# A conformer block on one core: the passage behind attention reordered, and its last token tile normalised from PSUM in halves

## The chip, the cores and the metric

The kernel runs on one core of one Trainium2 chip. The metric is the device time of one execution in microseconds (us); smaller is better. The profile of a kernel is taken from one execution of it. Its span is about 4 us shorter than the device time of the same execution, so I compare spans with spans and times with times.

## The reference

Input x is 2 x 4000 tokens of 512 features; the inner width of the feed-forwards is 2048, and the depthwise convolution has 3 taps. Norms have no learned factors.

```python
h = _layernorm(x);  h = _silu(h @ w_ff1_a) @ w_ff1_b;  x1 = x + 0.5 * h
h = _layernorm(x1); q, k, v = h @ w_q, h @ w_k, h @ w_v
p = _softmax(jnp.einsum('btd,bsd->bts', q, k) * scale)
x2 = x1 + jnp.einsum('bts,bsd->btd', p, v) @ w_o
h = _layernorm(x2) @ w_pw1
h = a * _sigmoid(b)                      # a, b: the two halves of h
dc = depthwise convolution of h over 3 tokens
dc = (dc - mu) / jnp.sqrt(var + 1e-05)   # mu, var over all tokens
x3 = x2 + _silu(dc) @ w_pw2
h = _layernorm(x3); h = _silu(h @ w_ff2_a) @ w_ff2_b; x4 = x3 + 0.5 * h
return _layernorm(x4)
```

The statistics of the convolution run over all tokens. So nothing behind them can start before the last tokens have left attention, and this is what makes a **passage** between attention and the second feed-forward in which TensorE has little work to choose from.

## The kernel before

Tokens are handled in chunks of four tiles of 127. TensorE (PE) does all products, and transposes the normed tiles. A norm is: statistics and mean on VectorE (DVE), variance plus EPS on DVE, power of -0.5 on GpSimd (POOL), a shift on DVE (minus mean times factor, one column), and the norm itself on ScalarE (ACT) or DVE. PSUM is the memory that PE's sums go to, in banks. The "gate" is the product of a and the sigmoid of b, on one engine, with copies of its edge columns for the neighbouring chunk (the halo); the "swish" is the silu behind the convolution, on ACT. SyncE (SP) and ACT issue the transfers (DMA).

```python
def copy_o(self, W):                       # attention output, PSUM to SBUF, 4 copies
    for dc in range(DC):
        if dc % 2: DVE tensor_copy(self.OT[:, dc, 0:W], self.Yb[dc][:, 0:W])
        else:      ACT Copy of the same
# ... project(g, ti): 4 matmuls of one tile from OT, then the residual on DVE

def gate(eng):                             # in conv_a, for the last but one chunk
    self.S.op(eng, lambda e: e.tensor_tensor(out=out, in0=asb, in1=th, op=ALU.mult), ...)
    self.halo_left(t, jj); self.halo_right(t, jj)      # two one-column copies on POOL
if jj < DC - 1:
    return gate("POOL")
return lambda: gate("DVE")

def ln_factor(self, sl, ti):
    # DVE: va = mv + EPS;  POOL: rs = va ** -0.5
```

The passage itself, first half (attention's end to the last tile's products) and second half (to the feed-forward):

```python
for jj in range(self.KEEP, DC - 2):
    self.conv_b(tail, jj)
    self.conv_a(tail, jj)
def prepare(ti):
    self.project(last, ti)
    if ti == 0: self.conv_b(tail, DC - 2)
    if ti == 2: self.conv_a(tail, DC - 2)
for ti in self.ln_tiles(last, ..., prepare, ("ACT", "ACT", "DVE", "DVE")):
    if ti == TPC - 3:
        self.conv_b(tail, DC - 1)
        gate = self.conv_a(tail, DC - 1)
# ... transposes of the normed tiles, gate(), copies of the depthwise products
# ... loop over the last chunk's channel groups
self.conv_shift(DC - 2); self.swish(0, 2)
self.pw2_x(0, all_t[0:2], banks[0:2])
finish(DC - 1)                             # depthwise products and statistics, last group
self.conv_shift(DC - 1); self.swish(0, 3)
# ... norms of the first chunk
ybanks = [ybank() for _ in all_t]
self.pw2_x(1, all_t, ybanks)               # five matmuls for each of four tiles
self.pw2(1, all_t, ybanks, False)
x_away(1, 0, "ACT"); x_away(1, 1, "DVE"); x_away(0, 0, "ACT")
for k in range(2):
    self.transpose_pair(k, 0, ("ACT", "DVE")[k], ybanks[k], 0)
# ... the other x_away copies, then the feed-forward
```

The end of the last chunk, and the end of the program. A second version of the program stands behind a branch and is not taken in these runs:

```python
for ti in range(token_tiles(c)):           # in ff_last
    for f in range(FC):                    # 16 matmuls of 512 columns
        self.ff_second(f, ti, *blocks[f], f == FC - 1)
    self.residual(self.Yb[ti][0:TILE, :], self.b_Y[ti], c * TPC + ti, 0.5)
    self.ln_stats(c, sl, ti); self.ln_mean(sl, ti); self.ln_factor(sl, ti)
    self.ln_norm(c, sl, ti, self.osb[0][:, ti, :], self.b_osb[0][ti], "DVE")
    self.store_out(c, self.osb[0], self.b_osb[0], ti, ti + 1, ("SP", "ACT"))
# ... in build()
self.program(False)
self.wait_out()
with nc.If(fits < 1):
    S.barrier(); self.program(True); self.wait_out()
```

The first weights are loaded in this order at the start (each piece of `w_a` is 256 KB):

```python
for k in range(self.NWA):
    self.load_wa(i["w_ff1_a"], k, "SP")
    self.load_wb(i["w_ff1_b"], 2 * k, 2 * k + 2)
```

Of the kernel before, what the change touches and what calls it, by code (L numbers as in the profile page):

```python
# [246 lines left out]
class Conformer:  # L247
# [19 lines left out]
    def memory(self):  # L267
# [70 lines left out]

        self.P = [C.view(oP + s * 1024, CHUNK) for s in range(self.NP)]
# [45 lines left out]

        ns = self.LN_SLOTS
# [10 lines left out]
        self.st = [small(TPC * 6, parts=TILE).rearrange("p (t s) -> p t s", t=TPC) for _ in range(ns)]  # L397
# [3 lines left out]
        self.va = [small(TPC, parts=TILE) for _ in range(ns)]  # L401
        self.b_va = [[Buf("va") for _ in range(TPC)] for _ in range(ns)]
# [9 lines left out]
        self.b_nr1 = Buf("nr1")  # L412
        self.onef = small(1)
# [196 lines left out]
    def ln_stats(self, c, sl, ti, src=None):  # L610
        x, b_x = self.tokens(c, ti, src)
        self.S.op("DVE", lambda e: e.bn_stats(self.st[sl][:, ti, :], x), reads=[b_x], writes=[self.b_st[sl][ti]])  # L612

    def ln_aggr(self, sl, n, shift=False):
        S = self.S
        for ti in range(n):
            S.op("DVE", lambda e, ti=ti: e.bn_aggr(self.mv[sl][:, ti, :], self.st[sl][:, ti, :]),
                 reads=[self.b_st[sl][ti]], writes=[self.b_mv[sl][ti]])
        S.op("DVE", lambda e: e.tensor_scalar(self.va[sl][:, 0:n], self.mv[sl][:, 0:n, 1], EPS, None, ALU.add),  # L619
             reads=self.b_mv[sl], writes=self.b_va[sl])  # L620
        S.op("POOL", lambda e: e.tensor_tensor(out=self.rs[sl][:, 0:n], in0=self.va[sl][:, 0:n],  # L621
                                               in1=self.neghalf[0:TILE, 0:n], op=ALU.pow),
             reads=self.b_va[sl] + [self.b_neghalf], writes=self.b_rs[sl])
# [98 lines left out]
    def ln_factor(self, sl, ti):  # L722
        S = self.S
        S.op("DVE", lambda e: e.tensor_scalar(self.va[sl][:, ti:ti + 1], self.mv[sl][:, ti, 1:2], EPS, None, ALU.add),
             reads=[self.b_mv[sl][ti]], writes=[self.b_va[sl][ti]])
        S.op("POOL", lambda e: e.tensor_tensor(out=self.rs[sl][:, ti:ti + 1], in0=self.va[sl][:, ti:ti + 1],  # L726
                                               in1=self.neghalf[0:TILE, ti:ti + 1], op=ALU.pow),
             reads=[self.b_va[sl][ti], self.b_neghalf], writes=[self.b_rs[sl][ti]])
# [64 lines left out]
    def ff_last(self, c, old):  # L793

        S, late = self.S, FC - self.NP
        blocks = []
# [11 lines left out]
        sl = self.nxt("ln", self.LN_SLOTS)  # L808
        for ti in range(token_tiles(c)):
            for f in range(FC):  # L810
                self.ff_second(f, ti, *blocks[f], f == FC - 1)
            self.residual(self.Yb[ti][0:TILE, :], self.b_Y[ti], c * TPC + ti, 0.5)
            self.ln_stats(c, sl, ti)
            self.ln_mean(sl, ti)
            self.ln_factor(sl, ti)
            self.ln_norm(c, sl, ti, self.osb[0][:, ti, :], self.b_osb[0][ti], "DVE")
            self.store_out(c, self.osb[0], self.b_osb[0], ti, ti + 1, ("SP", "ACT"))

# [178 lines left out]
    def copy_o(self, W):  # L997
        for dc in range(DC):
            if dc % 2:
                self.S.op("DVE", lambda e, dc=dc: e.tensor_copy(self.OT[:, dc, 0:W], self.Yb[dc][:, 0:W]),  # L1000
                          reads=[self.b_Y[dc]], writes=[self.b_OT[dc]])
            else:
                self.act(self.OT[:, dc, 0:W], self.Yb[dc][:, 0:W], AF.Copy, [self.b_Y[dc]], [self.b_OT[dc]])

    def project(self, g, ti):
# [3 lines left out]
        n, t0 = r.stop, ti * TILE - r.start  # L1009
        for dc in range(DC):  # L1010
            self.mm(ps[0:n, :], self.OT[:, dc, t0:t0 + n], self.Wvo[:, dc, :],
                    dc == 0, dc == DC - 1, [self.b_OT[dc], self.b_Wvo], b_ps)
# [11 lines left out]
    def finish_queries(self, g, done):  # L1024
        self.copy_o(width(g))
# [22 lines left out]
    def conv_a(self, t, jj):  # L1048
# [6 lines left out]
        if t == NCK - 2 and jj >= self.KEEP:  # L1055
# [10 lines left out]
            if jj < DC - 1:  # L1066
                return gate("POOL")
            return lambda: gate("DVE")
# [221 lines left out]
    def constants(self):  # L1290
        S = self.S
        S.op("POOL", lambda e: e.memset(self.neghalf, -0.5), writes=[self.b_neghalf])
        S.op("DVE", lambda e: e.memset(self.zero, 0.0), writes=[self.b_zero])  # L1293
        S.op("POOL", lambda e: e.memset(self.hl, 0.0), writes=self.b_hl)
        for j in range(TPC):
            S.op("DVE", lambda e, j=j: e.memset(self.ltm[j], 0.0), writes=[self.b_ltm[j]])
        S.op("POOL", lambda e: e.memset(self.onef, 1.0), writes=[self.b_onef])
        S.op("DVE", lambda e: e.memset(self.XT[SHARED][HALF - 32:HALF], 0.0), writes=[self.bx[SHARED]])
# [8 lines left out]
    def program(self, any_score):  # L1307
# [95 lines left out]
        for jj in range(self.KEEP, DC - 2):  # L1403
            self.conv_b(tail, jj)
            self.conv_a(tail, jj)

        def prepare(ti):
            self.project(last, ti)
            if ti == 0:
                self.conv_b(tail, DC - 2)  # L1410
            if ti == 2:
                self.conv_a(tail, DC - 2)

        for ti in self.ln_tiles(last, self.nxt("ln", self.LN_SLOTS), prepare, ("ACT", "ACT", "DVE", "DVE")):
            if ti == TPC - 3:
                self.conv_b(tail, DC - 1)
                gate = self.conv_a(tail, DC - 1)
# [4 lines left out]
        gate()  # L1422
# [8 lines left out]
        def finish(cc):  # L1431
            for t in (last, tail):
                f, copy = self.depthwise(t, cc)
                f()
                copies.append(copy)
            self.conv_scale(cc)
# [25 lines left out]
        self.conv_shift(DC - 2)  # L1462
        self.swish(0, 2)
# [3 lines left out]
        finish(DC - 1)  # L1467
# [15 lines left out]
        for ti in self.ln_tiles(0, self.nxt("ln", self.LN_SLOTS), None, ("ACT", "ACT", "DVE", "DVE"), x):  # L1483
            pass
        ybanks = [ybank() for _ in all_t]
        self.pw2_x(1, all_t, ybanks)
        self.pw2(1, all_t, ybanks, False)
# [7 lines left out]
        x_away(1, 1, "DVE")  # L1495
        x_away(0, 0, "ACT")
        for k in range(2):
            self.transpose_pair(k, 0, ("ACT", "DVE")[k], ybanks[k], 0)
        for t, ti, eng in ((0, 1, "ACT"), (0, 2, "DVE"), (1, 2, "ACT"), (0, 3, "DVE"), (1, 3, "ACT")):
# [78 lines left out]
```

## Time and profile before

| | before |
|---|---|
| median of the runs beside the changed kernel | 2047.64 us (4 runs, 2047.34 to 2047.93) |
| span of the profile | 2043.1 us |
| PE busy | 99% |
| idle PE time in the passage (1512 to 1556) | 5.8 us |
| last matmul's end to the end of the span | 5.8 us |

PE is busy in all but 13.5 us of 2043.1, so a change that takes no matmul away can win only part of these. The prediction below shows the lines of the page, the passage and the tail, and how they are read.

### The profile page before, as it was taken

The page shows a single profiled execution, that of the slowest core. Times are in us where ns is not written, and L with a number is a line of the kernel's source. Part 1 is how long each engine was busy: PE and PEld are TensorE (multiplying, and loading weights), DVE is VectorE, ACT ScalarE, POOL GpSimd, SP SyncE. Part 2 cuts the span into 40 slices and gives each one's busy share as a digit, 9 for nine tenths or more (in the row PEclk, how much of TensorE's full clock was granted, in tenths as well). Part 3 has the DMA queues.
Part 4 walks back from the last instruction along what each step waited for, and adds up shares of the span by engine and source line. Part 5 has one row for each costly group of instructions (what it writes and reads, how often), then busy time and mean ns, then how long its engine had stood idle before and what let it go on. Part 6 is the DMA issues. An engine that isn't in the chain of part 4 may idle for free.

```text
span 2043.1 us, 24518 instructions
## 1 busy us (share of the span) xinstructions
PE 2029.6 (99%) x9649; PEld 1028.9 (50%) x9649; DVE 1093.0 (54%) x2264; ACT 743.9 (36%) x1274; POOL 109.4 (5%) x236
## 2 busy tenths in 40 slices
PE   9999999999999999999999999999999999999998
PEld 5555555554444444445444444444445555555555
DVE  4244443334556667666766676667674444434434
ACT  3433333333333333333333333333345443443433
POOL 1000000000000000000000000000011000000000
PEclk9999999999999999999999999999999999999999
DMA  8222245320101111114421111111143111111111
GB/s 185 52 62 62 53 101 124 96 70 8 26 16 29 24 31 26 29 24 96 106 55 23 28 29 29 24 28 29 39 135 93 32 31 42 32 31 41 28 35 38
DMA packets 253121, 104.42 MB, mean 51 GB/s; under 512 B 193412, under 2 KB 252487, under 8 KB 252999
## 3 DMA queue, kind: packets, MB, share of 16 engines
q1 hardware_dynamic: 252751, 102.61, 21.1%
q8 instruction: 78, 1.28, 0.3%
q14 instruction: 44, 0.36, 0.1%
q10 hardware_dynamic: 248, 0.18, 0.0%
HBM read 33.77 MB, written 23.34 MB: 28 GB/s over the span
## 4 chain that ended last, share of the span: by engine, by line
PE 97%; DVE 1%; issue 0%; POOL 0%; DMA 0%; ACT 0%; POOLq 0%; SPq 0%; DVEq 0%; ACTq 0%
PE s L500 55%; PE y L500 42%; DVE work L612 0%; DVE wff L1177 0%; POOL work L726 0%; ACT work L550 0%; DVE xt L753 0%; DMA work<-work 0%; DMA xt<-in_x_dram 0%; DVE work L634 0%; POOL work L1186 0%; DVE work L547 0%; DVE wff L1071 0%; DVE work L920 0%; DVE work L719 0%
## 5 line engine op out<-in xcount | busy, mean ns | idle before, releaser
L550 ACT ACTIVATE work<-s 128x508 bf16<-128x508 f32 (+3 forms) x1060 | 621.7, 587 | 1212.8 <-PE s L500 1208.3
L500 PE MATMUL s<-work,wff 128*128 128x508 bf16 (+5 forms) x2624 | 628.2, 371 | 2.3 <-DVE work L547 1.8
L500 PE MATMUL s<-work,keys 128*128 128x508 bf16 (+1 forms) x2048 | 516.7, 374 | 0.1
L500 PE MATMUL y<-work,keys 128*128 128x508 bf16 (+2 forms) x2048 | 504.3, 373 | 0.4 <-DVE work L1000 0.4
L500 PE MATMUL y<-wff,work 128*127 128x512 bf16 x1992 | 501.2, 379 | 0.0
L920 DVE TENSOR_TENSOR work<-work 128x508 f32<-128x508 f32 (+2 forms) x496 | 334.6, 675 | 279.9 <-ACT work L550 278.8
L500 PEld LDWEIGHTS s<-work,wff 128*128 128x128 bf16 x2624 | 252.2, 98 | 278.6 <-issue 6.2
L500 PEld LDWEIGHTS y<-wff,work 128*127 128x127 bf16 x1992 | 273.7, 137 | 171.4
L500 PEld LDWEIGHTS s<-work,keys 128*128 128x128 bf16 x2048 | 199.5, 98 | 231.9 <-issue 0.6
L500 PEld LDWEIGHTS y<-work,keys 128*128 128x128 bf16 (+1 forms) x2048 | 193.5, 97 | 234.0 <-issue 6.2
L753 DVE SCALAR_TENSOR_TENSOR xt<-y,xt 127x512 bf16<-127x512 f32 x126 | 78.5, 683 | 360.1 <-PE y L500 360.1
L612 DVE BATCH_NORM_STATS2 work<-xt 127x6 f32<-127x512 bf16 x312 | 197.3, 680 | 6.3 <-DMA xt<-in_x_dram 6.2
L500 PE MATMUL s<-work 128*127 128x512 bf16 (+3 forms) x776 | 197.0, 378 | 2.2 <-DVE work L1293 1.2
L621 POOL TENSOR_TENSOR work<-work 127x4 f32<-127x4 f32 (+1 forms) x76 | 76.5, 1007 | 1133.0 <-DVE work L619 1133.0
L500 PEld LDWEIGHTS s<-work 128*127 128x127 bf16 (+1 forms) x776 | 94.9, 124 | 76.9 <-issue 3.7
L634 DVE TENSOR_SCALAR work<-xt,work 127x512 bf16<-127x512 bf16 x307 | 110.8, 407 | 26.2 <-POOL work L621 22.9
L753 DVE SCALAR_TENSOR_TENSOR xt<-s,xt 127x512 bf16<-127x512 f32 x55 | 38.0, 692 | 144.6 <-PE s L500 144.6
L753 DVE SCALAR_TENSOR_TENSOR xt<-s,work,xt 127x512 bf16<-127x512 f32 x64 | 48.0, 751 | 32.1 <-PE s L500 31.5
L1075 DVE SCALAR_TENSOR_TENSOR wff<-wff,s 128x508 bf16<-128x508 f32 (+1 forms) x57 | 38.7, 679 | 41.6 <-PE s L500 41.4
L550 ACT ACTIVATE wff<-s 128x508 f32<-128x508 f32 (+1 forms) x67 | 39.5, 591 | 55.1 <-PE s L500 55.1
L550 ACT ACTIVATE work<-keys,work 128x508 bf16<-128x508 bf16 (+1 forms) x68 | 52.3, 775 | 1.4 <-DVE work L1191 1.3
L1156 POOL COPY wff<-wff 128x1 bf16<-128x1 bf16 x56 | 10.4, 187 | 635.3 <-DVE wff L1075 632.8
(83 smaller groups left out, 424.5 us busy)
## 6 DMA issues: line engine op xcount, KB each, us to landing
keys<-keysd SPq DMA_DIRECT2D x62, 128.0 KB, 2.3
keysd<-work SPq DMA_DIRECT2D x14, 448.0 KB, 3.2
out_dram<-work SPq DMA_DIRECT2D x14, 448.0 KB, 3.2
dcvd<-wff SPq DMA_DIRECT2D x48, 127.0 KB, 1.7
keys<-dcvd SPq DMA_DIRECT2D x12, 508.0 KB, 4.9
xt<-in_x_dram SPq DMA_DIRECT2D x13, 448.0 KB, 4.8
wff<-in_w_ff_a_dram SPq DMA_DIRECT2D x16, 256.0 KB, 5.4
work<-work SPq DMA_TRANSPOSE x208, 2.5
```

Source lines behind the costliest of these rows:

```text
L500: self.S.op("PE", lambda e: e.matmul(out, lhsT, rhs, start=start, stop=stop, **kw), reads=reads, writes=[bank], inc=stop if inc is None el ...
L550: return self.S.op("ACT", lambda e: e.activation(out, in_, func, **kw), reads=reads, writes=writes)
L612: self.S.op("DVE", lambda e: e.bn_stats(self.st[sl][:, ti, :], x), reads=[b_x], writes=[self.b_st[sl][ti]])
L621: S.op("POOL", lambda e: e.tensor_tensor(out=self.rs[sl][:, 0:n], in0=self.va[sl][:, 0:n], in1=self.neghalf[0:TILE, 0:n], op=ALU.pow), rea ...
L634: self.S.op("DVE", lambda e: e.tensor_scalar(out, x, self.mv[sl][:, ti, 0:1], self.rs[sl][:, ti:ti + 1], ALU.subtract, ALU.mult), reads=[b ...
L753: self.S.op("DVE", lambda e: e.scalar_tensor_tensor(out=self.XT[g][rows], in0=ps[rows], scalar=scalar, in1=self.XT[g][rows], op0=ALU.mult, ...
L920: S.op("DVE", lambda e, p=p, n=n, acc=acc: e.tensor_tensor(out=acc, in0=acc, in1=self.P[p][0:n, 0:W], op=ALU.add), reads=[self.b_P[p], sel ...
L1075: self.S.op("DVE", lambda e: e.scalar_tensor_tensor(out=out, in0=th, scalar=1.0, in1=ps[:, 0:W], op0=ALU.add, op1=ALU.mult), reads=[b_ps, ...
L1156: S.op("POOL", lambda e: e.tensor_copy(self.G[gs][:, jj, 0:1], self.G[gp][:, jj, CHUNK:CHUNK + 1]), reads=[self.b_G[gp][jj]], writes=[self ...
```

## The change

The intent is to fill PE's idle time at both ends of the passage and behind the last matmul. It has five parts.

1. **EPS goes into the statistics.** The six numbers that DVE's statistics give for a tile are followed by three constant ones, which stand for no element but are to add D times EPS to the sum of squares in the operation that forms mean and variance. So the variance is to have EPS in it, and the 91 adds on DVE that the profile of before counts go.
2. **First half.** The copies of the attention output are split at 127 columns, so that the first tile is projected ahead of the gates' products; of the two gates on POOL the first stays, behind the first tile's power ("factor"), and the second goes to DVE, where the third was already.
3. **Second half.** The shift of the third channel group, which waits for POOL (DVE idles 0.73 us at 1542.28 before), stands behind a statistics operation instead of ahead of it.
4. **Second half.** Only three tiles of the second chunk are multiplied ahead of the transposes; the fourth tile's five matmuls come behind them, while their copies run. The first transposes get a spare PSUM bank.
5. **Tail.** PE adds twice the residual through an identity matrix, so that the last tile's sum is twice x4, whose norm is the same with four times EPS. The tile is done in two halves of 256 columns, with ACT's square root and DVE's reciprocal in place of POOL's power; one half is normed by DVE and one by ACT, from PSUM.

```diff
-    def copy_o(self, W):
+    def copy_o(self, g):
+        W = width(g)
+        for lo, hi, b_o in ((0, TILE, self.b_OT), (TILE, W, self.b_OTr)) if g == NCK - 1 else ((0, W, self.b_OT),):
+            for dc in range(DC):
+                self.away("DVE" if dc % 2 else "ACT", self.OT[:, dc, lo:hi], self.Yb[dc][:, lo:hi], self.b_Y[dc], [b_o[dc]])
@@ conv_a
-            if jj < DC - 1:
-                return gate("POOL")
-            return lambda: gate("DVE")
+            return gate
@@ ln_factor (and the same in ln_aggr)
-        S.op("DVE", lambda e: e.tensor_scalar(self.va[sl][:, ti:ti + 1], self.mv[sl][:, ti, 1:2], EPS, None, ALU.add), ...)
-        S.op("POOL", lambda e: e.tensor_tensor(out=self.rs[sl][:, ti:ti + 1], in0=self.va[sl][:, ti:ti + 1], ...
+        S.op("POOL", lambda e: e.tensor_tensor(out=self.rs[sl][:, ti:ti + 1], in0=self.mv[sl][:, ti, 1:2], ...
@@ constants
+        for sl in range(self.LN_SLOTS):
+            S.op("DVE", lambda e, sl=sl: e.memset(self.st[sl][:, :, 6:8], 0.0), writes=self.b_st[sl])
+            S.op("DVE", lambda e, sl=sl: e.memset(self.st[sl][:, :, 8:9], D * EPS), writes=self.b_st[sl])
@@ first half
-        for jj in range(self.KEEP, DC - 2):
-            self.conv_b(tail, jj)
-            self.conv_a(tail, jj)
+        self.conv_b(tail, DC - 3)
+        fill = [None, lambda: gates.append(self.conv_a(tail, DC - 3)), lambda: self.conv_b(tail, DC - 2),
+                lambda: gates.append(self.conv_a(tail, DC - 2))]
         def prepare(ti):
             self.project(last, ti)
-            if ti == 0:
-                self.conv_b(tail, DC - 2)
             if ti == 2:
-                self.conv_a(tail, DC - 2)
+                gate("POOL")
+            if fill[ti]:
+                fill[ti]()
 ...
+        gate("DVE")
         drains = [self.depthwise(tail - 1, self.KEEP)]
 ...
-        gate()
+        gate("DVE")
@@ second half
-        self.conv_shift(DC - 2)
-        self.swish(0, 2)
         self.pw2_x(0, all_t[0:2], banks[0:2])
-        finish(DC - 1)
+        def between():
+            self.conv_shift(DC - 2)
+            self.swish(0, 2)
+        finish(DC - 1, between)
 ...
-        self.pw2_x(1, all_t, ybanks)
-        self.pw2(1, all_t, ybanks, False)
+        spare = ybanks.pop()
+        self.pw2_x(1, all_t[0:3], ybanks)
+        self.pw2(1, all_t[0:3], ybanks, False)
+        ybanks.append(ybanks[1])
 ...
-        x_away(1, 1, "DVE")
-        x_away(0, 0, "ACT")
-        for k in range(2):
-            self.transpose_pair(k, 0, ("ACT", "DVE")[k], ybanks[k], 0)
+        x_away(1, 1, "ACT")
+        self.transpose_pair(0, 0, "DVE", spare, 0)
+        self.transpose_pair(1, 0, "DVE", ybanks[0], 0)
+        self.pw2_x(1, all_t[3:], ybanks[3:])
+        self.pw2(1, all_t[3:], ybanks[3:], False)
@@ ff_last, last tile
+        for m, (ps, b_ps, d) in enumerate(halves):
+            self.mm(ps[0:TILE, d], self.two[0:TILE, 0:TILE], self.XT[g][:, d], True, False, ...)
+            for f, (p, b_p) in enumerate(blocks):
+                self.mm(ps[0:TILE, d], p[:, ti * TILE:(ti + 1) * TILE], self.Wb[:, f, d], False, f == FC - 1, ...)
+            S.op("DVE", lambda e, m=m, ps=ps, d=d: e.bn_stats(st[:, m, 0:6], ps[0:TILE, d]), ...)
+ ...    # bn_aggr, ACT Sqrt (bias 2 * EPS), DVE reciprocal, shift, DVE norms half 0, ACT half 1
+        self.store_out(c, self.osb[0], b_o, ti, ti + 2, ("SP", "ACT"))
```

## The prediction

> **What bounds the kernel now.** I read the page first: busy shares and the chain that ended last.
>
> ```profile
> span 2043.1 us, 24518 instructions
> ...
> PE 2029.6 (99%) x9649; PEld 1028.9 (50%) x9649; DVE 1093.0 (54%) x2264; ACT 743.9 (36%) x1274; POOL 109.4 (5%) x236
> ...
> PE 97%; DVE 1%; issue 0%; POOL 0%; DMA 0%; ACT 0%; POOLq 0%; SPq 0%; DVEq 0%; ACTq 0%
> ```
>
> TensorE sets the time nearly everywhere, and the change takes no matmul away (it adds two). So it can only win where PE stands still. Windows show PE at 100% from 13 to 400 us, 99.9% from 400 to 1400 and 100% from 1556 to 2026. What is left lies in three places: the head (0 to 12 us), the passage behind attention (1512 to 1556) and the tail (2037 to the end). Nothing done to DVE elsewhere can be seen in the time.
>
> The passage, from the timeline of PE alone:
>
> ```profile
> 1526.09 0.39 PE L528 MATMUL y<-work 127*128 127x127 bf16 x4
> 1527.61 1.08 PE L528 MATMUL y<-work 127*128 127x127 bf16 x12 [1.13 <-ACT work L550]
> 1528.52 0.81 PE L500 MATMUL y<-wff 128*128 128x508 bf16 x3
> 1529.62 1.66 PE L500 MATMUL s<-work,wff 128*128 128x444 bf16 x8 [0.29 <-DVE work L547]
> ...
> 1542.57 2.91 PE L500 MATMUL s<-work 128*127 128x512 bf16 x12
> 1546.51 1.08 PE L500 MATMUL s<-work 128*127 128x512 bf16 x4 [1.03 <-ACT work L550]
> ...
> 1552.03 0.62 PE L528 MATMUL y<-work 127*128 127x127 bf16 x8
> 1552.98 0.62 PE L528 MATMUL y<-work 127*128 127x127 bf16 x8 [0.33 <-DVE xt L547]
> 1554.48 4.48 PE L500 MATMUL s<-work,wff 128*128 128x508 bf16 x20 [0.88 <-DVE work L547]
> ```
>
> [...] I count start to next start instead, less the number of matmuls by their pitch: 0.216 us for 508 or 512 columns, 0.187 for 444, 0.055 for 127. Four transposes at 1526.09 should end the slot at 1526.31; the next start is 1527.61: 1.30 lost. In the same way, in order: 0.25 and 0.45 up to 1529.62, 0.24 at 1531.36, 0.35 at 1540.91, 1.35 up to 1546.51, 0.29 before 1552.03, 0.51 before 1552.98, 1.06 before 1554.48. Sum 5.8 us.
>
> Why 1.30: the norm of tile 1 on ACT came late, and the full timeline shows one reason.
>
> ```profile
> 1523.73 1.26 POOL L1061 TENSOR_TENSOR wff<-wff 128x508 bf16<-128x508 f32 x1 [0.22 <-ACT wff L550]
> ...
> 1524.22 0.78 DVE L672 SCALAR_TENSOR_TENSOR work<-work 127x1 f32<-127x1 f32 x1
> ...
> 1526.55 0.15 DVE L672 SCALAR_TENSOR_TENSOR work<-work 127x1 f32<-127x1 f32 x1
> ```
>
> A one-column DVE operation takes 0.15 us, but 0.78 when POOL's gate runs; it ends with the gate (1525.00 and 1524.99). Tile 1's power on POOL also stood behind that gate, from 1524.31 (its input ready) to 1525.31.
>
> The tail:
>
> ```profile
> 2035.39 1.89 PE L500 MATMUL y<-wff,work 128*127 128x512 bf16 x8
> ...
> 2037.32 0.69 DVE L753 SCALAR_TENSOR_TENSOR xt<-y,xt 127x512 bf16<-127x512 f32 x1 [0.54 <-PE y L500]
> 2038.04 0.69 DVE L612 BATCH_NORM_STATS2 work<-xt 127x6 f32<-127x512 bf16 x1
> ...
> 2038.99 0.15 DVE L724 TENSOR_SCALAR work<-work 127x1 f32<-127x1 f32 x1
> 2039.22 0.55 POOL L726 TENSOR_TENSOR work<-work 127x1 f32<-127x1 f32 x1 [2.89 <-DVE work L724]
> 2039.81 0.41 DVE L634 TENSOR_SCALAR work<-xt,work 127x512 bf16<-127x512 bf16 x1 [0.66 <-POOL work L726]
> ```
>
> PE ends at 2037.28, the last norm at 2040.22, the store and the end take 2.9 more.
>
> [...]
>
> **Passage, first half.** Copies of the attention output are split at 127 columns, so tile 0 is projected one group of matmuls earlier. PE reaches it at 1516.80 + 4 x 0.216 = 1517.66; the short copies start at 1516.90, take about 0.27 each[...] and are done by 1517.5. No wait; the long parts (about 0.45 each) end by 1518.3, before tile 1 at 1518.52. Residual 0 then runs from 1518.70 (was 1519.67). DVE from there: stats 0 to 1520.2, residual 1 to 1520.85, mean 0 at 1520.75, so POOL's power 0 from 1521.0 to 1521.55. Only now comes the one gate left on POOL, 1521.6 to 1522.9, two halo copies, power 1 to 1523.75. DVE: residual 2, stats 2 to 1522.95, shift 0 at 1523.0 (the gate is over), residual 3, stats 3, shift 1 at 1524.5. ACT norm 0 1523.1 to 1523.9, norm 1 1524.6 to 1525.45. PE, with the same matmuls in front of it, comes to the transposes at 1526.07: norm 1 is there, the 1.30 is gone, and so is the 0.25 (norm 3 on DVE ends near 1525.7). The two gates moved to DVE cost 0.68 each; one stands at 1525.7 while DVE would idle, the other behind the copies of the transposes as before. Copies: second pair transposed by 1526.93, DVE 0.75 to 1527.85, so the first matmuls of the last tile start at 1528.0 instead of 1529.62. **Gain 1.6.** The loop behind it is not changed, nor its 0.24 and 0.35.
>
> **Second half.** Statistics of the last tile no longer stand behind a shift that waits for POOL: DVE idles 0.73 us at 1542.28 in front of it; one stats (0.67) goes into that hole. The last swish, and PE's 1546.51, come 0.67 earlier: 1545.84. Norms of tile 0 start as much earlier and lose one small add per tile (about 0.07 each), ending at 1551.1 on DVE. ACT sets the rest: swishes of tile 1 at 0.72 each, from 1546.6 to 1549.6, norms 0 and 1 to 1550.8. PE now does three tiles, 0.65 a group, so it waits some 0.35 in all for the swishes, ends at 1550.35, waits for norm 1 to 1550.95 (0.6). The first transposes go to a spare bank and wait for no copy; the second at 1551.4; the fourth tile's five matmuls (1.08) start when its bank is copied, 1551.85, and end at 1552.93. Meanwhile DVE copies the transposes (0.69 each, was 1.02 on ACT for one) to 1552.8. The feed-forward starts at 1552.95 instead of 1554.48. **Gain 1.5**, of it 1.08 the five matmuls.
>
> **Tail.** 34 matmuls of 256 columns take 3.69 instead of 3.45, two of them (adding 2x by an identity) new: PE ends at 2037.5, 0.2 later. Then stats of one half 0.41[...], mean 0.2, ACT square root 0.3, reciprocal 0.18, shift 0.15, ACT identity on 256 columns 0.50, with some 0.3 between engines: 2039.5 instead of 2040.22. **Gain 0.75.** Residual, 0.69 us stats and POOL's 0.55 go.
>
> **Head.** The add of EPS (0.15 us, 0.2 with its step) leaves the chain to the first matmuls twice, so ACT's first copy would come 0.35 earlier. But the second weight piece, issued at 4.44, lands 3.9 us later, 8.34, and its matmuls run at 8.55 now: **gain 0.15**. Eight small memsets on DVE end before the input lands at 3.57.
>
> Sum: 1.6 + 1.5 + 0.75 + 0.15 = 4.0. 2047.35 - 4.0 = **2043.3 us**.
>
> **Rivals.** (a) The waits only change their names: power 1 stands behind the gate on POOL still, and ACT's swishes and norms hold PE in the second half. For it: ACT is busy almost without a gap from 1547 to 1554. Against: 0.6 us of slack at norm 1. Then only the five matmuls and the tail stay: 2045.3. (b) An earlier feed-forward meets its weights: the last piece lands at about 1557.3. Against: the loads are issued when PE frees their room, so they come earlier too, and the first piece lands near 1552.4 for a use at 1558.8. It would take back all of the passage: 2046.4. (c) The tail's five small steps on two engines cost as much as the two long ones: 2044.1. (d) More than 80 adds less on DVE speed the middle: PE doesn't wait there, so nothing.
>
> **Range and chances.** The run-to-run spread is 0.6 us. (a) in part or (c) lifts by about 1, a head without its limit lowers by 0.2: 2042.3 to 2045.0. 2% is 41 us, far more than all idle time of PE, so the same within 2% is near certain.
>
> **What would show it.** Right: transposes behind attention start without a wait near 1526; the first 444-column group near 1528.0; feed-forward 3.1 us earlier after the head's shift is taken off; last norm 2.0 us after PE's end. Wrong: PE waiting over 1 us for ACT at either transposes, DMA as a releaser after the passage, a second table load in the tail.

The sum came to 1.6 + 1.5 + 0.75 + 0.15 = 4.0. What the trace of before has for the figures:

- A row of eight matmuls of 512 columns lasts 1.89 us, 0.16 more than eight pitches of 0.216. So starts are compared.
- The short copies' 0.27: ACT takes 0.540 us for 444 columns and 0.593 for 508, DVE 0.613 and 0.678. Carried on to 127 columns that is 0.28 and 0.29 (estimates).
- The 3.69 for 34 matmuls of 256 columns: the head's sixteen of 254 columns have a pitch of 0.109, so 34 take 3.7.
- The 0.41 for the statistics of a half: DVE takes 0.620 us for 444 columns from PSUM and 0.690 for 508, which carried on to 256 gives 0.41 (an estimate).
- The 0.3 of the square root, the 0.50 of ACT's norm and that the tail needs just one table load were estimates, which the trace of before does not show.

## The result and the profile after

The changed kernel took **2044.35 us** (median of 4 runs, 2043.36 to 2045.05) beside 2047.64 (4 runs, 2047.34 to 2047.93) for the kernel before: a ratio of 0.9984 (95% interval 0.9966 to 1.0001), the same within 2%. A ratio is the mean time of one kernel's fast runs over that of the other's of the same rounds, so it is not quite the ratio of the medians. The interval alone doesn't rule out that nothing was gained; but the slowest of the four runs is 2.3 us faster than the fastest of the kernel before. The prediction was 2043.3, with 2042.3 to 2045.0 as its range. All outputs are right.

The page of the changed kernel; its first line is the span, the second the busy time of each engine, the third the shares of the chain that ended last:

```profile
span 2040.1 us, 24550 instructions
...
PE 2029.2 (99%) x9665; PEld 1029.8 (50%) x9667; DVE 1081.1 (53%) x2187; ACT 746.9 (37%) x1280; POOL 107.7 (5%) x235
...
PE 98%; DVE 1%; ACT 0%; DMA 0%; SPq 0%; POOL 0%; issue 0%; DVEq 0%; ACTq 0%
```

PE's work is the same to 0.4 us and the span is 3.0 us shorter: all that was won is idle time of PE. DVE has 77 instructions and 12 us less, which shows nowhere by itself.

The passage, timeline of PE in the changed kernel (start, busy us, what, and in brackets the idle time ahead of it and its releaser):

```profile
1526.10 1.06 PE L534 MATMUL y<-work 127*128 127x127 bf16 x16
...
1528.09 1.66 PE L506 MATMUL s<-work,wff 128*128 128x444 bf16 x8 [0.17 <-DVE work L553]
...
1541.04 2.91 PE L506 MATMUL s<-work 128*127 128x512 bf16 x12
1544.36 1.08 PE L506 MATMUL s<-work 128*127 128x512 bf16 x4 [0.41 <-ACT work L556]
...
1549.40 1.10 PE L534 MATMUL y<-work 127*128 127x127 bf16 x12 [0.25 <-ACT work L556]
1550.37 0.43 PE L506 MATMUL y<-xt,work 127*127 127x512 bf16 x1
1550.64 1.03 PE L506 MATMUL y<-work 128*127 128x512 bf16 x4
1551.50 4.48 PE L506 MATMUL s<-work,wff 128*128 128x508 bf16 x20
```

All sixteen transposes run in one piece from 1526.10; before, they stood 1.13 us in the middle. The last tile's products start at 1528.09 instead of 1529.62. The last swish still holds PE at 1544.36, less than before, and the fourth tile's five matmuls (1550.37 to 1551.50) now fill the time in which the transposes are copied. Why ACT came in time for the transposes, from the timeline of all engines:

```profile
1521.59 1.26 POOL L1092 TENSOR_TENSOR wff<-wff 128x508 bf16<-128x508 f32 x1
1522.90 0.14 DVE L676 SCALAR_TENSOR_TENSOR work<-work 127x1 f32<-127x1 f32 x1
```

The shift of the first tile now starts when POOL's gate is over, and takes 0.14 us instead of 0.78.

The tail:

```profile
2033.54 1.04 PE L506 MATMUL y<-wff,work 128*127 128x256 bf16 x8
2034.61 0.43 DVE L832 BATCH_NORM_STATS2 work<-y 127x6 f32<-127x256 f32 x1 [0.57 <-PE y L506]
...
2035.35 0.29 ACT L556 ACTIVATE work<-work 127x1 f32<-127x1 f32 x1 [9.36 <-DVE work L833]
...
2035.95 0.54 DVE L845 TENSOR_SCALAR work<-y,work 127x256 bf16<-127x256 f32 x1
2036.07 0.56 ACT L556 ACTIVATE work<-y,work 127x256 bf16<-127x256 f32 x1 [0.42 <-DVE work L841]
```

PE ends at 2034.57 and the last norm at 2036.63, 2.06 us later; it was 2.94. But the span ends at 2040.06, 3.43 us behind the last norm; it was 2.84.

To hold traces against each other I cut each at five points of PE's timeline. **Head**: start of the first 254-column product. **Middle**: from there to the row sums behind the last value products. **P**: from the last sixteen value products (1512.83) to the first 444-column product. **Q**: from there to the feed-forward. **T**: from the last tile's first matmul to the end of the last norm. **U**: from there to the end of the span. The stretch between Q and T is 479.19 us in every trace. The middle reaches 3.00 us into P, so the parts add up to the span only when these are taken off.

| trace | head | middle | P | Q | T | U | span | gained |
|---|---|---|---|---|---|---|---|---|
| before | 11.12 | 1504.71 | 16.79 | 24.86 | 6.56 | 2.84 | 2043.06 | |
| after | 11.33 | 1504.51 | 15.26 | 23.41 | 5.94 | 3.43 | 2040.06 | 3.00 |
| gained | -0.21 | 0.20 | 1.53 | 1.45 | 0.62 | -0.59 | | 3.00 |

### The profile page after: what moved, and what is told of

The parts are those of the page before. It is cut to its first block, busy times and chain, and to the rows that moved or that the text cites. A ratio compares the mean times of both kernels' runs of the same rounds, so it can differ in the third digit from the quotient of the medians.

```text
span 2040.1 us, 24550 instructions
## 1 busy us (share of the span) xinstructions
PE 2029.2 (99%) x9665; PEld 1029.8 (50%) x9667; DVE 1081.1 (53%) x2187; ACT 746.9 (37%) x1280; POOL 107.7 (5%) x235
## 3 DMA queue, kind: packets, MB, share of 16 engines
q8 instruction: 78, 1.28, 0.3%
## 4 chain that ended last, share of the span: by engine, by line
PE 98%; DVE 1%; ACT 0%; DMA 0%; SPq 0%; POOL 0%; issue 0%; DVEq 0%; ACTq 0%
PE s L506 56%; PE y L506 42%; ACT work L556 0%; DVE wff L1206 0%; DMA wff<-in_w_ff_a_dram 0%; SPq L568 0%; POOL work L1215 0%; DVE work L553 0%; DVE wff L1100 0%; PE y L534 0%; ACT keys L556 0%; DVE work L1213 0%; SPq L560 0%; DVE work L869 0%; DVE work L952 0%
## 5 line engine op out<-in xcount | busy, mean ns | idle before, releaser
L506 PE MATMUL y<-wff,work 128*127 128x512 bf16 (+1 forms) x2000 | 501.4, 378 | 0.0
```

The source lines that it names most:

```text
L506: self.S.op("PE", lambda e: e.matmul(out, lhsT, rhs, start=start, stop=stop, **kw), reads=reads, writes=[bank], inc=stop if inc is None el ...
```

## The experiments

Eleven more kernels ran, the first of them the changed kernel once more. Their times are medians of fast runs, each with its ratio to the kernel before. With 4 or 5 runs each the times separate about 1 us; most parts are smaller than that, so the verdicts on the parts rest on the cuts of the traces, which the first experiment tests for how well they repeat.

| kernel | time us (range) | ratio (95%) | head | P | Q | T | U |
|---|---|---|---|---|---|---|---|
| after_again | 2044.46 (2044.20 to 2045.00) | 0.9986 (0.9973 to 1.0000) | 11.14 | 15.25 | 23.40 | 5.94 | 3.95 |
| old_tail | 2044.05 (2043.48 to 2044.62) | 0.9983 (0.9968 to 0.9998) | 11.90 | 15.25 | 23.41 | 6.45 | 2.87 |
| gate_early | 2045.35 (2044.98 to 2046.31) | 0.9992 (0.9976 to 1.0007) | 10.84 | 16.68 | 23.41 | 5.94 | 3.35 |
| old_project | 2044.90 (2044.10 to 2045.31) | 0.9988 (0.9972 to 1.0003) | 11.50 | 16.13 | 23.25 | 5.94 | 3.06 |
| shift_first | 2044.79 (2044.25 to 2045.10) | 0.9986 (0.9971 to 1.0002) | 11.20 | 15.26 | 24.03 | 5.94 | 3.89 |
| four_at_once | 2045.23 (2044.31 to 2047.58) | 0.9993 (0.9978 to 1.0008) | 11.52 | 15.26 | 23.76 | 5.94 | 3.20 |
| weights_first | 2043.63 (2043.10 to 2044.53) | 0.9982 (0.9968 to 0.9996) | 11.03 | 15.26 | 23.39 | 5.94 | 3.42 |
| whole_tail | 2044.02 (2043.37 to 2044.11) | 0.9982 (0.9969 to 0.9996) | 11.87 | 15.26 | 23.40 | 6.17 | 2.66 |
| eps_only | 2046.55 (2046.27 to 2046.71) | 0.9996 (0.9980 to 1.0011) | 11.60 | 16.60 | 24.40 | 6.45 | 2.70 |
| best | 2043.35 (2043.11 to 2043.59) | 0.9980 (0.9966 to 0.9994) | 11.00 | 15.25 | 23.40 | 6.17 | 2.78 |
| best_copies | 2042.72 (2042.68 to 2043.15) | 0.9977 (0.9964 to 0.9991) | 10.92 | 15.26 | 22.99 | 6.17 | 2.64 |

The kernel before took 2047.29 in the call of the first four, 2047.60 in that of the next four and 2047.43 in that of the last three (nine runs each). The middle is 1504.49 to 1504.53 in all eleven.

### after_again: what repeats

No edit; the changed kernel once more.

> The changed kernel once more, word for word, as a control. It is to show what of the trace repeats. In the first trace PE waited 0.36 us in the head for the second weight piece (issued 4.44, landed 4.3 us later; 3.9 before the change), waited 0.31 us at 1498 for a DMA transpose (0.52 before), and the end came 3.43 us after the last compute (2.84 before). Theory (structure): all three repeat within 0.1 us, because each follows from the order of the instructions. Rival (chance of the DMA): the landing in the head and the end differ by 0.3 us or more from the first trace. The passage and the last tile's compute (5.94 us from its first matmul to the last norm's end) should repeat within 0.1 either way. Time: 2044.3 plus or minus 0.5, ratio to before 0.9984.

P, Q and T came again within 0.01 us. Head (0.19 lower) and U (0.52 higher) did not. The wait at 1498 repeated too (the middle is 1504.51 in both). So for the head and the end the rival holds, and for the rest the theory: the second weight piece landed 3.8 us after its issue here, and 4.3 in the first trace. Differences of P, Q and T of some hundredths count, and single values of head and U do not. T and U together were 9.40 before, and 9.37 and 9.89 in the two traces of the changed kernel: its tail gained nothing that can be shown.

### old_tail: the last tile as before

```diff
-        ti, g = n - 1, c * TPC + n - 1
-        st, b_st = ...              # the whole block of two halves
+        for ti in range(token_tiles(c)):   # loop of the kernel before, for the last tile too
```

> The changed kernel with the last tile as before (whole, residual, POOL's power), all else changed. Theory: from the last tile's first matmul to the last norm's end 6.56 less the 0.2 of the add of EPS, so 6.35, against 5.94; the end then comes 2.8 us later as in the kernel before, because the store no longer meets PE's last instruction fetch (one 16 KB packet of 1.42 us lay on the store's packets in the changed kernel). Together 9.15 to 9.2 against 9.37 in the changed kernel: the halves of the last tile gave nothing in the end, the two kernels' times are equal within 0.3 us. Rival: the late landing was chance, then the end is 0.4 us later than that of the changed kernel.

The load of the square root's table and the doubled identity go with the block. T went up by 0.51 to 6.45 (0.11 under the kernel before, which still adds EPS, and 0.1 above what I expected), and U came down to 2.87. T and U are 9.32 together, not more than the 9.37 and 9.89 of the changed kernel, and the time is 2044.05 beside 2044.46. So the tail's new form won compute time and lost as much behind the last norm. The loss is in the landing of the store, which the view of DMA issues for the last microseconds shows (KB each, and us from issue to landing). Before:

```profile
out_dram<-work SPq DMA_DIRECT2D x1, 112.0 KB, 2.6
out_dram<-work ACTq DMA_DIRECT2D x1, 15.0 KB, 2.1
```

After, the same view, with its line of instruction fetches:

```profile
q8 instruction: 1, 0.02, 1.8%
...
out_dram<-work SPq DMA_DIRECT2D x1, 112.0 KB, 3.2
out_dram<-work ACTq DMA_DIRECT2D x1, 15.0 KB, 3.0
```

The same bytes land 0.6 and 0.9 us later, and a 16 KB fetch of instructions (queue q8) stands in the window, which has none of this size in the kernel before. (Fetches of 8 KB, queue q14, stand in both windows.) The trace's records of single packets tell when. In this list times are us from the end of the last norm; the store is 127 packets of 1 KB, and each 16 KB fetch is one packet. eps_only, told below, has the old tail too.

```
               first fetch   second fetch, its end    half the store   last packet
before            -4.80        -1.62     -0.68            1.27            1.60
old_tail          -4.72        -1.61     -0.28            1.26            1.61
eps_only          -5.25        -1.93     -0.98            1.26            1.62
after             -2.59         0.51      1.93            1.24            2.63
after_again       -2.59         0.90      2.39            1.25            3.15
```

(The middle of the store is 1.24 to 1.27 in all traces.) Where the second fetch ends ahead of the store, the last packet lands at 1.6; where it falls into the store, at 2.6 or 3.2, while the first half of the packets is not touched. The span ends 0.8 us behind the last packet in the changed kernel and 1.2 before.

The records of PE's sequencer, which the trace keeps apart from the array's matmuls, say when the fetches move. At the end of the program it comes to the branch, which begins with a load: at 2033.25 before and at 2032.46 after, while the array ends at 2037.28 and 2034.57. So the sequencer is 4.0 us ahead of the array with matmuls of 512 columns and 2.1 us ahead with 256. At 0.216 and 0.109 us a matmul that is 19 matmuls in both. With half as long matmuls the branch came about half as early ahead of the end. The two fetches go with it: in all thirteen traces the first starts 1.03 to 1.62 us behind the branch's start, the branch ends 1.26 to 1.49 us behind that fetch's end, and the second fetch starts 0.77 to 1.31 us behind the branch's end.

### whole_tail: the new chain, whole columns

If that is the cause, the new chain with matmuls of 512 columns must keep most of its gain.

```diff
-        halves = [(self.Yb[k], self.b_Y[k], slice(m * D // 2, (m + 1) * D // 2)) for m, k in enumerate((0, ti))]
-        for m, (ps, b_ps, d) in enumerate(halves):
+        ps, b_ps = self.Yb[ti], self.b_Y[ti]      # one identity matmul and 16 of 512 columns
         ...
-                # half 0 on DVE, half 1 on ACT
+        self.ln_norm(c, sl, ti, self.osb[0][:, ti, :], self.b_osb[0][ti], "DVE", {ti: (ps[0:TILE, :], b_ps)})
-        S.op("POOL", lambda e: e.memset(self.eps2, 2 * EPS), writes=[self.b_eps2])
+        S.op("POOL", lambda e: e.memset(self.eps2, 3 * EPS), writes=[self.b_eps2])
```

(The statistics of two halves hold the constants twice and so 2 EPS, those of one piece once; the square root's bias adds what is missing to 4.)

> The changed kernel with the last tile in one piece, but without residual, POOL's power and the add: matmuls of 512 columns (one adds 2x), statistics on the bank, square root on ACT, reciprocal and norm on DVE. Theory (PE's sequencer is some 19 matmuls ahead of the array, so with 512 columns it meets its branch 4.0 us before PE's end and its two instruction fetches are over before the store; with 256 columns only 2.0 us before, and the second fetch falls on the store): compute from the last tile's first matmul 6.2 us (6.56 before, 5.94 in halves), the end 2.85 us later (3.06 to 3.95 in four traces with halves, 2.84 and 2.87 in two without); in sum 9.05 against 9.4 to 9.9. Rival (the late store comes from the square root's or the two engines' waits before it, not from PE's fetch): the end is 3.1 to 3.9 us later here too, sum 9.3 to 10.

```profile
2033.16 1.89 PE L506 MATMUL y<-wff,work 128*127 128x512 bf16 x8
...
2035.09 0.70 DVE L830 BATCH_NORM_STATS2 work<-y 127x6 f32<-127x512 f32 x1 [0.86 <-PE y L506]
...
2036.58 0.81 DVE L638 TENSOR_SCALAR work<-y,work 127x512 bf16<-127x512 f32 x1
```

One statistics and one norm of 512 columns cost 0.70 and 0.81 where the halves cost 0.43 and 0.56 on the path. So T, with the identity matmul in it, is 6.17: 0.23 more than in halves, 0.28 less than old_tail. The fetches came 4.79 and 0.74 us ahead of the last norm's end, the second took 1.01, and the last packet landed at 1.81. U is 2.66 and the sum 8.83, better than the 9.05 expected, and better than every trace in halves (9.00 to 9.89 in seven, 9.41 in the mean) and in the old form (9.40 before, 9.32 in old_tail, 9.15 in eps_only). The two kernels built on it below give 8.95 and 8.81.

So two edits moved the fetch (old_tail, whole_tail), and the last packet went with it. The other traces agree: in each of the five further ones in halves the second fetch starts 0.53 to 1.07 us behind the last norm and the last packet lands at 2.22 to 3.12, and in each of the six without halves it starts ahead of it and the last packet is at 1.60 to 1.98. The closest sign is this: in all seven traces in halves the last packet lands 0.69 to 0.76 us behind the end of the second fetch, wherever between 1.52 and 2.39 that end lies, and 12 to 15 of the 127 packets land later than 1.62, the latest packet of the three old tails. So I read the fetch as what holds these packets up. It isn't shown outright: how the two meet in the DMA engines the traces don't tell, and I could not move the fetch alone. Two things are left over. In whole_tail, best and best_copies 4 or 5 packets are late as well (last packet at 1.78 to 1.98), without a 16 KB fetch beside them; an 8 KB one ends 0.48 to 0.57 us ahead of the last of them. And from the last packet to the end of the span it takes 0.72 to 0.86 us in the ten traces with the new chain (square root and reciprocal), but 1.08 to 1.27 in the three with the old one, for which the traces give no reason. That, and not the packets, is why U is 0.21 shorter in whole_tail than in old_tail.

In time, whole_tail's 2044.02 isn't distinct from the changed kernel's.

### gate_early: two gates on POOL as they come

```diff
-        fill = [None, lambda: gates.append(self.conv_a(tail, DC - 3)), lambda: self.conv_b(tail, DC - 2),
-                lambda: gates.append(self.conv_a(tail, DC - 2))]
+        fill = [None, lambda: self.conv_a(tail, DC - 3)("POOL"), lambda: self.conv_b(tail, DC - 2),
+                lambda: self.conv_a(tail, DC - 2)("POOL")]
         ...
-            if ti == 2:
-                gate("POOL")
-        gate("DVE")
```

> The changed kernel with its new projection order, but gates 1 and 2 on POOL at once as before, in front of the LayerNorm powers. Measure: from the start of the last sixteen value matmuls to the first 444-column group of the last tile (16.79 us before, 15.25 changed). Theory (the powers behind the gates made the wait): POOL's power 0 waits for gate 1 until 1522.65, power 2 for gate 2 until 1526.3, norms 2 and 3 come 1.4 us later, the measure is 16.4 to 16.7. Rival (the earlier projection alone made the gain): 15.25 to 15.5.

P is 16.68, 1.43 more, as expected in size: the wait of PE for ACT's norm of tile 1 is back in the midst of the transposes. The expectation had named norms 2 and 3, held up by the powers. It is the one-column shift of tile 1 on DVE that is late: it lasts as long as POOL's second gate runs.

```profile
1524.49 1.26 POOL L1092 TENSOR_TENSOR wff<-wff 128x508 bf16<-128x508 f32 x1 [1.07 <-ACT wff L556]
1524.59 1.18 DVE L676 SCALAR_TENSOR_TENSOR work<-work 127x1 f32<-127x1 f32 x1
...
1526.67 0.86 PE L534 MATMUL y<-work 127*128 127x127 bf16 x8 [0.66 <-ACT work L556]
```

Nothing else of the passage is moved (Q 23.41). So the first half rests on the place of the gates.

### old_project: the gate's products ahead of the first tile, copies whole

```diff
-        self.conv_b(tail, DC - 3)
         gates = []
+        self.conv_b(tail, DC - 3)
+        gates.append(self.conv_a(tail, DC - 3))
-        fill = [None, lambda: gates.append(...DC - 3), lambda: self.conv_b(tail, DC - 2), lambda: gates.append(...DC - 2)]
+        fill = [lambda: self.conv_b(tail, DC - 2), None, lambda: gates.append(self.conv_a(tail, DC - 2)), None]
-        for lo, hi, b_o in ((0, TILE, self.b_OT), (TILE, W, self.b_OTr)) if g == NCK - 1 else ((0, W, self.b_OT),):
+        for lo, hi, b_o in ((0, W, self.b_OT),):
```

> The changed kernel with the gates behind the powers, but the projection of tile 0 one group of matmuls later and the copies of the attention output unsplit, as before. Same measure (16.79 before, 15.25 changed). Theory (the two parts work in a row: residual 0 starts 0.9 us later, at 1519.67, and with it norm 1; the slack at the transposes was some 0.5 us): a wait of 0.3 to 0.6 at the first transposes, the measure is 15.6 to 16.0. Rival 1 (only the gates matter): 15.25 to 15.4. Rival 2 (only the projection matters): 16.6 and more.

P is 16.13, 0.88 more: above what I expected, and far from what the two rivals said. The part beyond is a second wait that I had not counted, of the depthwise products for the halo copies that POOL does behind the gate:

```profile
1528.48 0.82 PE L506 MATMUL y<-wff 128*128 128x508 bf16 x3 [0.57 <-POOL wff L1195]
```

So both the early projection (with the split copies, which were not tested apart from it) and the place of the gates are needed. Their 0.88 and 1.43 are together more than the 1.53 gained: they work in a row, and either one missing costs a part of the same time.

### shift_first: the shift that waits for POOL back in front

```diff
+        self.conv_shift(DC - 2)
+        self.swish(0, 2)
         self.pw2_x(0, all_t[0:2], banks[0:2])
-        def between(): ...
-        finish(DC - 1, between)
+        finish(DC - 1)
```

> The changed kernel, but the shift of the third channel group and its swish stand again in front of the statistics of the last group, as before. Measure: from the first 444-column group of the last tile to the start of the feed-forward, 24.86 us before and 23.41 changed. Theory: the last swish comes 0.62 us later and the whole chain behind it (ACT's copies, swishes, norms) with it: 24.0 to 24.1. Rival: the later wait of PE for the norms takes it up, 23.4 to 23.6.

Q is 24.03, 0.62 more, as expected, and the wait that PE has for the last swish is larger by 0.63 (0.41 in the changed kernel):

```profile
1544.85 1.08 PE L506 MATMUL s<-work 128*127 128x512 bf16 x4 [1.04 <-ACT work L556]
```

### four_at_once: all four tiles ahead of the transposes

The block between `ybanks` and the feed-forward as in the kernel before (the edit is the reverse of that part of the diff above).

> The changed kernel, but the second tile's pointwise matmuls for all four token tiles at once ahead of the transposes, no spare bank, copies of the transposes as before. Same measure (24.86 before, 23.41 changed). Theory (PE only waits elsewhere: before the change 1.06 us stood in front of the feed-forward; part of what the five moved matmuls fill comes back as waits for ACT's swishes and norms): 24.1 to 24.3, so the part is worth 0.7 to 0.9 and with the shift's 0.62 makes up the 1.45. Rival: it is worth the full 1.08 of the five matmuls, 24.5.

Q is 23.76, only 0.35 more. I had expected 0.7 to 0.9, and the rival more still; both missed, on the same side. (One of its four runs took 2047.58 us at a clock of 0.998, the widest spread of all; the traced one took 2044.31.)

```profile
1550.05 1.10 PE L534 MATMUL y<-work 127*128 127x127 bf16 x16
1552.03 1.24 PE L506 MATMUL s<-work,wff 128*128 128x508 bf16 x5 [0.88 <-DVE work L553]
```

Here all sixteen transposes run without a wait, and PE stands 1.1 us behind them, as in the kernel before. In the changed kernel PE comes to the transposes 1.29 us earlier (1548.76; 0.17 of it is the head of these two traces), finds that one of ACT's norms is not there, and waits 0.42 at 1549.40 and 0.31 more at 1550.37, for the copy that frees the fourth tile's bank. (Each is start to start, less four and twelve transposes by 0.055.) It then has no wait left behind its five matmuls. So 1.10 us of waiting became 0.73, a gain of 0.37, near the 0.35 of Q.

### eps_only: the kernel before without the adds

```diff
-        self.st = [small(TPC * 6, ...
+        self.st = [small(TPC * 9, ...
+        ... memsets of columns 6 to 8
-        S.op("DVE", ... EPS, None, ALU.add) ...   # twice; POOL's power reads mv
```

> The kernel before with one part of the change alone: EPS as a third record of the statistics instead of an add on DVE ahead of each power. Theory (the add was on two paths that I had taken to be off PE's): the wait for the DMA transpose at 1498 falls from 0.71 to 0.50 us between starts, and from the first 254-column group to the sums behind attention it is 1504.5 us as in all nine traces with the change, not 1504.7; in the second half of the passage the norms of the first tile come about 0.3 us earlier, 24.4 to 24.6 instead of 24.86; the first half stays at 16.7 to 16.8 (gate and POOL's power hold it). Rival (the adds were hidden; the 0.2 at 1498 comes from another part): 0.7, 1504.7, 24.86.

P is 16.60 (0.19 less than before), Q 24.40 (0.46 less), T 6.45 (0.11 less), the middle 1504.51 (0.20 less). So the smallest part works in four places. In Q a wait of 0.51 us in the midst of the transposes is gone (1552.98 before), and all sixteen run in one piece:

```profile
1552.11 1.11 PE L528 MATMUL y<-work 127*128 127x127 bf16 x16
```

This completes the sum: 0.62 (shift), 0.35 (fourth tile) and 0.46 (EPS) give 1.43 of the 1.45 gained. That they add up is no accident of the order: for Q, four_at_once is eps_only with the shift moved, and its 23.76 is 0.64 under 24.40, beside the 0.62 of shift_first. The 0.20 of the middle, for which the prediction had nothing, is one wait. Timeline of PE near 1498, before:

```profile
1498.36 1.89 PE L500 MATMUL s<-work,wff 128*128 128x508 bf16 x8 [0.35 <-DMA work<-work]
```

and after:

```profile
1498.36 1.89 PE L506 MATMUL s<-work,wff 128*128 128x508 bf16 x8 [0.15 <-issue]
```

PE waits there for the transpose of a normed tile by DMA. In the changed kernel PE came to it 0.21 us later (its head was late by as much), and yet the same products start at the same time: the chain of the norm ahead of the transpose is shorter by the add. The start to start times give 0.52 us lost before, 0.31 after and 0.30 in eps_only.

### weights_first: the head's second weight piece earlier

The head of the changed kernel waits for a weight piece, which is issued third:

```diff
+        self.load_wa(i["w_ff1_a"], 0, "SP")
+        self.load_wa(i["w_ff1_a"], 1, "SP")
         for k in range(self.NWA):
-            self.load_wa(i["w_ff1_a"], k, "SP")
+            if k > 1:
+                self.load_wa(i["w_ff1_a"], k, "SP")
             self.load_wb(i["w_ff1_b"], 2 * k, 2 * k + 2)
```

> The changed kernel, with the first two pieces of the first weight loaded ahead of the second weight's first piece. Six traces so far have the start of the ninth head matmul at 8.28 to 9.33 us and the first 254-column group 2.57 us later each time; the rest of the kernel follows it (that group to the sums at the end of attention: 1504.5 us in all four traces with the change, to 0.03). Theory (the second piece's landing sets the head): issued 0.5 us earlier, it lands before PE needs it, the ninth matmul starts at 8.2 to 8.3, the 254-column group at 10.8, the time falls by 0.3 to 0.6 us. Rival (the landing is set by all that is in flight, not by the order of issue): spread as before, 10.8 to 11.9, no gain.

The changed kernel's head, timeline of PE:

```profile
8.75 0.62 PE L506 MATMUL s<-work,wff 128*128 128x127 bf16 x8 [0.36 <-DMA wff<-in_w_ff_a_dram]
```

With the piece issued second:

```profile
8.02 1.05 PE L506 MATMUL s<-work,wff 128*128 128x127 bf16 x16 [0.17 <-ACT work L556]
```

PE no longer waits for the DMA, and its start is now set by ACT's copy, near 8.0. Without the edit the landing sets the head: in eight of the ten traces with the old order it comes 2.62 to 2.64 us behind the landing of this piece, which took 3.8 to 4.8 us from its issue (before and after_again, with early landings, are the other two). The head is 11.03, somewhat later than the 10.8 expected. In the three kernels with this order it is 10.92 to 11.03; in the nine traces of other kernels than before without it, 10.84 to 11.90, with a mean of 11.4. The worth, some 0.4 us, is thus more a narrower spread than a shorter best case. The time, 2043.63, overlaps with the changed kernel's runs.

### best and best_copies: a better version

best is weights_first and whole_tail together. best_copies has in addition the copies of the last channel group's depthwise products on DVE instead of ACT. In best ACT does them from 1543.88 to 1544.88, ahead of the second chunk's swishes, while DVE idles 1.37 us:

```diff
-    def depthwise(self, t, cc, ring="Y"):
+    def depthwise(self, t, cc, ring="Y", eng="ACT"):
         ...
-                lambda: self.act(self.dcv[t][cc][:, 0:W], ps[:, 0:W], AF.Copy, [b_ps], [self.b_dcv[t][cc]]))
+                lambda: self.away(eng, self.dcv[t][cc][:, 0:W], ps[:, 0:W], b_ps, [self.b_dcv[t][cc]]))
         ...
-                f, copy = self.depthwise(t, cc)
+                f, copy = self.depthwise(t, cc, eng="DVE" if cc == DC - 1 else "ACT")
```

> The changed kernel with both remedies: the first two weight pieces loaded first, the last tile in one piece. Theory: 254-column group at 10.9 to 11.1, last tile and end together 8.83 us from its first matmul (9.37 to 9.9 in halves), span 2039.2, time 2043.2, some 1.2 us below the changed kernel and 4.2 below the kernel before. Rival (one of the two gains was chance): span 2039.7 to 2040.

> As the run before, and the two copies behind the last statistics on DVE, which idles 1.5 us there, instead of on ACT, whose swishes and norms then set the pace. Theory (ACT's chain sets the second half): ACT's swishes start 0.9 us earlier, then DVE's norms become the bound; first 444-column group to feed-forward 22.9 to 23.1 instead of 23.40. Rival (DVE's norm chain sets it already): 23.3 to 23.5.

best took 2043.35 us (2043.2 expected) and best_copies 2042.72, whose Q is 22.99, inside the range expected and 0.41 below best's. All five runs of best_copies (2042.68 to 2043.15) are faster than all nine of the changed kernel (2043.36 to 2045.05), though those ran in other calls. It is the fastest of all, by 4.7 us under the kernel before; about 2.4 us of PE's idle time in the passage are left (5.8 less 1.53, 1.45 and 0.41).

## Why the prediction was right or wrong

The prediction held: 2044.35 for 2043.3, inside the range. Its sum of 4.0 us is 3.0 in the traces. Both halves of the passage came as worked out; the tail and the head brought nothing, and 0.2 us came from where nothing was expected. Step by step:

- **First half, 1.6 predicted: 1.53.** The working is confirmed point by point: transposes at 1526.10 without a wait, the last tile's products at 1528.09 for 1528.0, the shift at 0.14 us when POOL's gate is over, the short parts of the split copies at 0.27 to 0.29 us each for 0.27. gate_early and old_project show that the place of the gates and the early projection carry it, each with the other. Rival (a), the power behind the gate still, is refuted here.
- **Second half, 1.5 predicted: 1.45.** The timeline is right: with the first half's 1.53 taken off, it has the last swish at 1544.31 (measured 1544.36), the transposes at 1548.82 (1548.76), the five matmuls at 1550.32 (1550.37) and the feed-forward at 1551.42 (1551.50), with waits for norm 1 and for a bank on the way. The shares are not: "Gain 1.5, of it 1.08 the five matmuls" failed. four_at_once shows 0.35 for them, since 0.73 turned into these very waits. This is rival (a), in part. The rest came from the shift, 0.62 for the 0.67 predicted, and from the missing adds, 0.46, for which the working had only about 0.07 a tile.
- **Tail, 0.75 predicted: 0.03 and -0.49 in the two traces of the changed kernel**, and -0.01 in the mean of the seven traces with its tail. The compute came nearly as predicted: PE 0.26 longer for the 0.24, the statistics of a half 0.43 for 0.41, the square root 0.29 for 0.3, ACT's norm of a half 0.56 for 0.50, last norm 2.06 behind PE's end for 2.0, one table load (1.28 us, at 2024.49) and none on the path; T is 0.62 shorter. The step that failed is "the store and the end take 2.9 more", taken as fixed. It was 3.43 and 3.95. With matmuls of 256 columns the branch at the program's end came 2.1 us ahead of PE's end instead of 4.0, and the second instruction fetch behind it 0.51 and 0.90 us behind the last norm, into the store, instead of 1.62 ahead of that norm. old_tail and whole_tail show that the late packets come and go with the fetch. Rival (c), five small steps as dear as two long ones, gave 2044.1, near the 2044.35 measured, but that is a coincidence: by T the steps are 0.62 cheaper.
- **Head, 0.15 predicted: -0.21 and -0.02.** The limit was named rightly, the landing of the second weight piece, but its 3.9 us were taken as fixed: it took 4.3 in this trace, and heads spread over 1.06 us with the same order of loads.
- **Middle, nothing predicted: 0.20.** "PE doesn't wait there, so nothing" (rival (d)) missed the one wait at 1498, which was in the profile of before as 0.35 for a DMA, and which eps_only shows to shorten.
- **Rival (b)**, weights that an earlier feed-forward meets, is refuted: the stretch from the feed-forward to the last tile is 479.19 us in every trace.

What stays open: by what path the instruction fetch holds up single packets of the store (or whether something else that goes with it does), why the end comes sooner behind the last packet with the new chain, and why the weight piece's landing spreads.

## What to carry to other kernels

When matmuls are moved into a hole, ask what else in that hole was ready early only because PE came late: here 0.73 of the 1.08 us moved became waits for ACT and for a bank. An end that "always takes 2.9 us" is made of something: here smaller matmuls at the very end moved the branch from 4.0 to 2.1 us ahead of the array's end, and with it a fetch of instructions from 1.62 us ahead of the last norm's end to 0.51 behind it, into the last store, whose last packet landed at 2.63 us instead of 1.60. Where a change is worth a few microseconds in two thousand, cut the traces at fixed points of the engine that sets the time and repeat one kernel first, to learn which of the cuts repeat to 0.01 us (here P, Q and T) and which are chance (head and U, 0.19 and 0.52 apart).
